# The product with w_in of blocks 1 and 0 by quarters, and the weights' sums made in block 1

## The chip, the core and the metric

The kernel runs on one core of one Trainium2 chip. The metric is device time in microseconds, the median of the runs shown. The engines: PE (TensorE, products; PEld its weight loads), DVE (VectorE), ACT (ScalarE), POOL (GpSimd), SP (SyncE, which issues most DMAs). Each engine takes its instructions in the order of its own queue.

## What is computed

```python
state = gamma * state + k_t v_t          # 4 batches, 8 heads, 768 steps, head size 64
y_t = scale * q_t state
x = y as (3072 tokens, 512)
xn = x / sqrt(mean(x*x) + 1e-6) * rms_g
x = (silu(xn @ w_gate) * (xn @ w_val)) @ w_out        # inner width 1536
h = x @ w_in                                          # 512 -> 1024
e = exp(h - max(h));  sm = e / (sum(e) + 1e-9)
solu = h * sm
ln = (solu - mean(solu)) / sqrt(var(solu) + 1e-6) * g_ln
out = ln @ w_out2                                     # 1024 -> 512
```

All in fp32. On PE a value is split into a high and a low part of type fp32r, and a product takes three matmuls: high by high, high by low, low by high.

## The kernel before

The 3072 tokens go in six blocks of 512. For a block there are these stages. *Attention* (`att_pieces`): per chunk of tokens a group of scores (rq by rk into the PSUM banks SB and YB), masks on DVE (L262, into A), and a group of outputs into the same banks (qd by U, A by rv, then rv by kd for the state); ACT copies the outputs into xT (L317) and squares them (L321). POOL makes qd (L241), kd (L236), the decay of U (L311), the scaling of xT (L322) and zeroes A (L264). *Norm* (`rms_steps`): DVE transposes and sums the squares (L390, L391), PE sums them over partitions (L392), DVE adds the epsilon (L393), POOL takes the root (L394), DVE spreads it (L397), POOL scales xT in four parts (L400), ACT makes the high parts xnh and POOL the low parts xnl (L101). *Values* (`bc_block`): for m from 0 to 11 the products with w_gate (bank GB) and w_val (bank VB), silu on ACT (L819), the multiplication on DVE (L790), a split, and the product with w_out (`cmm`) into the banks X0 to X3, which stand as X_68 to X_71 in the order below.

*Second half.* `de_quarters` (blocks 2 to 5) makes the product with w_in from four quarters of X and of the weights with seven products instead of eight; it needs sums of the weights' quarters: T1 (in two w4 tiles), T2 and T3 (in xnh and xnl, free once the values are done), and T4 (in w2["h"], w2["l"]). `de_block` (blocks 1 and 0) makes it straight, 96 matmuls a block: four groups of 128 tokens, each followed by its softmax. `soft` is the softmax: two maxima on DVE (L989), two exponentials on ACT (L992), on the last group a load of ACT's function table (L995), two multiplications on DVE (L997), and the mean taken off, half on DVE and half on POOL (L1002). `t_tr` transposes the result on PE (L1013), ACT makes the high part (L1016) and DVE the low part (L1017); ACT squares (L1020), and POOL makes the scale of a row with five short instructions (L1024 to L1028), a root among them (L1027). `e_mm` is the product with w_out2, 24 matmuls a group; ACT takes it out with the scale (L1053) and sends it away (L1054).

Block 0's second half runs after block 1's: at the end of block 0's values X goes to DRAM (`x2_store`), and comes back with `x2_load`. So the order is: block 0's values, block 1's values, block 1's second half, block 0's second half, block 2, and so on. Attention and norm of block n+1 are spread over block n's stages: a dictionary `extra` holds functions by (block, slot), `slot(n, s)` runs them, and slots 0 to 34 lie in the values, 35 and more in the second half. For block 2 they lie in the second halves of blocks 1 and 0, from slot 35 on.

The weights' sums: `w2_sums` runs in block 2's values. POOL puts high and low parts together (L601, 128x1024), takes four differences per half (L607), ACT and DVE split them, and SP stores them to `t2scr` in eight stores; `t_load` loads them in each block by quarters.

A scheduler orders the instructions of each engine from the program's order, its own reckoning of time and the marks `issue_after` and `high_priority`.

Of the kernel before, what the change touches and what calls it, by code (L numbers as in the profile page):

```python
# [9 lines left out]
F32 = mybir.dt.float32  # L10
# [13 lines left out]
NK = 4  # L24
# [12 lines left out]
SUMS_AT = [(2, 17), (2, 24)] + [(n, 1 + 6 * i) for n in (3, 4) for i in range(5)]  # L37
W2_SUMS_AT = (2, 9)
FIRST7 = 2
# [3 lines left out]
def retention_moe_kernel(ctx: ExitStack, tc: tile.TileContext, qk0, q2, kt, kv, wpk, w2i, w2o,  # L43
# [550 lines left out]
    def w2_sums(k):  # L594

        W, o = [], []
# [12 lines left out]
        def tied(hi, lo, t):  # L609
            with tc.issue_after(recent["act"].ins), tc.issue_after(recent["dve"].ins):  # L610
                split(hi, lo, t)

        def parts():
            for t in (W[0][:, 0, :], W[1][:, 1, :]):
                o.append(wt("x2", [P, 2, 512], F32R, 4))
                tied(o[-1][:, 0, :], o[-1][:, 1, :], t)

        def parts2():
            tied(w2["h"][:, k, 512:], w2["l"][:, k, 512:], W[1][:, 0, :])
            h, l = (wt("st", [P, 512], F32R, 3) for _ in range(2))  # L620
            tied(h, l, W[0][:, 1, :])
            o.extend((h, l))

        def store():
            for i in range(2):
                nc.sync.dma_start(t2scr[i][:, :, k, :], o[i].bitcast(F32))

        def store2():
            for i in range(2):
                nc.sync.dma_start(t2scr[2][:, i, k, :], o[2 + i].bitcast(F32))  # L630

        def none():
            pass

        return [whole, none, sums, none, parts, parts2, store, store2]
# [172 lines left out]
    def bc_block(n):  # L808
# [28 lines left out]
        if n >= FIRST7:  # L837
            t_load(1, n), t_load(2, n)
# [241 lines left out]
    def t_load(i, n):  # L1080
# [4 lines left out]
        for a in range(2):  # L1085
            nc.sync.dma_start(T1[a].bitcast(F32), t2scr[0][:, a])

    T1 = []

    def de_quarters(n, base):  # L1090

        V, S = nc.vector, nc.scalar

# [6 lines left out]
        for k in range(2):  # L1100
            split(a11[:, 0, k, :], a11[:, 1, k, :], XB[k][:, lo])
            S.copy(s1[:, k, :], XB[k][:, hi])
        for k in range(2):
            V.tensor_tensor(out=s3[:, k, :], in0=XB[k][:, lo], in1=s1[:, k, :], op=ALU.subtract)
        for k in range(2):
            split(xh[:, k, :], xl[:, k, :], XB[2 + k])
# [6 lines left out]
        for k in range(2):  # L1113
            i = V.tensor_tensor(out=s2[:, k, :], in0=XB[2 + k][:, hi], in1=s3[:, k, :], op=ALU.subtract)
# [365 lines left out]
```

## Time and profile before

| | |
|---|---|
| median of 3 runs | 979.44 us (978.98, 979.44, 981.68) |
| profiled execution | 982.31 us |
| its span | 980.4 us, mean granted clock of TensorE 0.991 of full speed |
| DMA over the span | 227.65 MB, mean 232 GB/s |

The profile shows one execution. The span runs from the first to the last instruction. A row of the timeline gives start and duration of an instruction; "x4" joins four in a row, with their time together; what stands in brackets is the idle time of the engine before it, and what ended it. PE's durations overlap, since matmuls are pipelined.

### The profile page before, as it was taken

Reading aid. Unit: us, or ns where it says so; the run is one execution under the profiler, and the core shown is the slowest. Engines: PE = TensorE matmul, PEld = TensorE weight load, DVE = VectorE, ACT = ScalarE, POOL = GpSimd, SP = SyncE. Lnnn points to the kernel's source line nnn. Section 1 sums busy time; section 2 is a strip of 40 time slices with the busy share of each in tenths; the row PEclk is TensorE's granted clock in tenths of the full one; section 3 lists DMA queues with packets and bytes.
Section 4 is the critical chain, followed back from the end, with each engine's and each line's share of the span. In section 5 each row is a group of like instructions: output and inputs, shape, how many; then the busy total and the mean of one; then the engine's idle time right before and its main releaser. Section 6 shows DMA issues by size and latency. Waiting matters only on the chain.

```text
span 980.4 us, 16072 instructions
## 1 busy us (share of the span) xinstructions
PE 966.5 (99%) x5868; PEld 805.4 (82%) x5868; DVE 504.6 (51%) x996; ACT 422.9 (43%) x824; POOL 447.1 (46%) x533
## 2 busy tenths in 40 slices
PE   8899999999999999999999999999999999999998
PEld 7778887888888888888888888888888888899987
DVE  4787785562364653433574233476323456344473
ACT  3766665573335443322455222356312256321354
POOL 6886775572053496443427335528242426300022
PEclk8899999999999999999999999999999999999999
DMA  9699999896612215898833789961698954698501
GB/s 348 225 325 391 347 319 372 324 340 226 200 42 83 70 43 180 279 312 282 294 117 108 278 295 346 300 196 67 205 341 294 322 190 140 230 324 295 193 1 44
DMA packets 94991, 227.65 MB, mean 232 GB/s; under 512 B 10816, under 2 KB 36800, under 8 KB 93888
## 3 DMA queue, kind: packets, MB, share of 16 engines
q1 hardware_dynamic: 86128, 201.44, 60.5%
q10 hardware_dynamic: 8784, 25.17, 6.6%
q8 instruction: 47, 0.77, 0.3%
q14 instruction: 32, 0.26, 0.1%
HBM read 184.63 MB, written 41.94 MB: 231 GB/s over the span
## 4 chain that ended last, share of the span: by engine, by line
PE 90%; POOL 3%; DMA 2%; DVE 2%; ACT 2%; issue 1%; SPq 0%; ACTq 0%; POOLq 0%; DVEq 0%
PE X L771 11%; PE X L773 10%; PE X L772 10%; PE GB L771 7%; PE GB L773 7%; PE GB L772 6%; PE VB L771 6%; PE VB L773 6%; PE VB L772 6%; PE SB L119 3%; PE X L1145 3%; PE GB L1145 2%; PE VB L1145 2%; PE YB L119 2%; PE VB L883 2%; PE YB L883 2%
## 5 line engine op out<-in xcount | busy, mean ns | idle before, releaser
L790 DVE TENSOR_TENSOR f<-VB,f 128x512 f32<-128x512 f32 x60 | 41.4, 690 | 131.4 <-PE VB L773 117.6
L772 PE MATMUL X<-r,wo 128*128 128x512 f32 x260 | 101.7, 391 | 0.0
L773 PE MATMUL X<-r,wo 128*128 128x512 f32 x260 | 101.4, 390 | 0.0
L771 PE MATMUL X<-r,wo 128*128 128x512 f32 x260 | 99.9, 395 | 0.0
L819 ACT ACTIVATE f<-GB 128x512 f32<-128x512 f32 x60 | 35.7, 596 | 144.4 <-PE GB L773 141.4
L100 ACT CAST r<-f 128x512 fp32r<-128x512 f32 x72 | 44.5, 619 | 118.5 <-DVE f L790 100.3
L672 POOL TENSOR_TENSOR st<-st,x 128x512 int32<-128x512 int32 x52 | 70.3, 1356 | 48.7 <-DVE st L671 10.6
L771 PE MATMUL GB<-xnh,w 128*128 128x512 f32 (+1 forms) x220 | 86.6, 394 | 1.5 <-ACT xnh L378 1.0
L771 PE MATMUL VB<-xnh,w 128*128 128x512 f32 (+1 forms) x220 | 86.0, 391 | 0.0
L772 PE MATMUL GB<-xnl,w 128*128 128x512 f32 (+1 forms) x220 | 85.7, 390 | 0.3 <-DVE xnl L101 0.2
L773 PE MATMUL VB<-xnh,w 128*128 128x512 f32 (+1 forms) x220 | 85.6, 389 | 0.0
L772 PE MATMUL VB<-xnl,w 128*128 128x512 f32 (+1 forms) x220 | 85.5, 389 | 0.0
L773 PE MATMUL GB<-xnh,w 128*128 128x512 f32 (+1 forms) x220 | 85.4, 388 | 0.0
L101 DVE TENSOR_TENSOR r<-f,r 128x512 fp32r<-128x512 f32 x72 | 61.7, 858 | 32.6 <-ACT r L100 32.1
L567 POOL TENSOR_TENSOR x<-x 128x512 f32<-128x512 f32 x24 | 31.5, 1319 | 95.6 <-DMA x<-scr 95.3
L101 POOL TENSOR_TENSOR r<-st,r 128x512 fp32r<-128x512 f32 x8 | 10.9, 1360 | 107.1 <-ACT r L100 104.9
L771 PE MATMUL X<-w2oh,r 128*128 128x512 f32 (+1 forms) x144 | 57.2, 397 | 1.1 <-ACT f L1053 0.6
L773 PEld LDWEIGHTS X<-r,wo 128*128 128x128 f32 x260 | 48.8, 188 | 10.2
L771 PEld LDWEIGHTS X<-r,wo 128*128 128x128 f32 x260 | 48.7, 188 | 10.2 <-ACT r L100 0.2
L772 PEld LDWEIGHTS X<-r,wo 128*128 128x128 f32 x260 | 48.8, 188 | 9.9 <-issue 0.2
L773 PE MATMUL X<-w2oh,r 128*128 128x512 f32 (+1 forms) x144 | 55.6, 386 | 0.0
L772 PE MATMUL X<-w2ol,r 128*128 128x512 f32 (+1 forms) x144 | 55.3, 384 | 0.0
(452 smaller groups left out, 2472.7 us busy)
## 6 DMA issues: line engine op xcount, KB each, us to landing
w<-scr SPq DMA_DIRECT2D x96, 512.0 KB, 4.9
wo<-scr SPq DMA_DIRECT2D x59, 512.0 KB, 5.2
x<-in_wpk SPq DMA_DIRECT2D x36, 512.0 KB, 6.2
x<-scr SPq DMA_DIRECT2D x25, 512.0 KB, 6.0
sscr<-x SPq DMA_DIRECT2D x24, 512.0 KB, 7.9
scr<-CV ACTq DMA_DIRECT2D x18, 512.0 KB, 6.2
rv<-in_kv SPq DMA_DIRECT2D x24, 256.0 KB, 4.4
scr<-w ACTq DMA_DIRECT2D x12, 512.0 KB, 4.6
```

What stands on the lines that cost most here:

```text
L100: h = nc.scalar.copy(hi, src)
L101: (lo_eng or nc.vector).tensor_tensor(out=lo, in0=src, in1=hi.bitcast(F32), op=ALU.subtract)
L119: return lambda: nc.tensor.matmul(out, lhsT=lhsT, rhs=rhs, start=start, stop=stop)
L567: nc.gpsimd.tensor_tensor(out=w[:, 0, :], in0=w[:, 0, :], in1=w[:, 1, :], op=ALU.add)
L672: nc.gpsimd.tensor_tensor(out=ti, in0=ti, in1=lo, op=ALU.add)
L771: nc.tensor.matmul(ps, lhsT=lh, rhs=rh, start=start, stop=False)
L772: nc.tensor.matmul(ps, lhsT=lh, rhs=rl, start=False, stop=False)
L773: return nc.tensor.matmul(ps, lhsT=ll, rhs=rh, start=False, stop=stop)
L790: recent["dve"] = nc.vector.tensor_tensor(out=a, in0=GV[1], in1=silu[:, 0, :], op=ALU.mult)
L819: recent["act"] = nc.scalar.activation(s[:, 0, :], GV[0], AF.Silu)
L883: nc.tensor.matmul(ps, lhsT=x, rhs=y[:, k, :], start=start and k + i == 0, stop=k == 1 and i == 2, skip_group_check=True)
L1145: last["mm"] = nc.tensor.matmul(bank, lhsT=x[:, k, ts_], rhs=y[:, k, :], start=start and k + i == 0, stop=k == 1 and i == 2, skip_group_ch ...
```

## The change

`FIRST7` becomes 1, so that blocks 1 and 0 go through `de_quarters` as well; block 0 takes X from DRAM with `x2_back` (two r2 tiles and one x2 tile). `w2_sums` moves to block 1's values, slots 27 to 33; T1 and T4 are split there, T2 and T3 by `w2_rest` into xnh and xnl behind the last product with w_val. They are used from there for blocks 1 and 0 without a load, and `w2_store` stores them once (two stores of 512 KB, two of 1 MB). Block 2's attention pieces are spread over slots 35 to 67 instead of 35 to 56, its norm steps over slots 72 to 77 instead of 57 to 64, and block 2's first weights are loaded at slots 39, 71 and 72. The sums of `SUMS_AT` are four each in blocks 2, 3 and 4.

```diff
--- before.py
+++ after.py
@@ -34,9 +34,9 @@
 CHAIN = 12
 W2_AT = [36 + 2 * j for j in range(16)]
 SEVEN = (5,)
-SUMS_AT = [(2, 17), (2, 24)] + [(n, 1 + 6 * i) for n in (3, 4) for i in range(5)]
-W2_SUMS_AT = (2, 9)
-FIRST7 = 2
+SUMS_AT = [(n, s) for n in (2, 3, 4) for s in ((3, 10, 17, 24) if n == 2 else (1, 8, 15, 22))]
+W2_SUMS_AT = (27, 29)
+FIRST7 = 1
 
 
 @with_exitstack
@@ -593,7 +593,7 @@
 
     def w2_sums(k):
 
-        W, o = [], []
+        W = W2s[k]
 
         def whole():
             for r in (k, k + 2):
@@ -606,33 +606,28 @@
             for out, a, b in ((b11, b12, b11), (b12, b22, b12), (b22, b22, b11), (b21, b21, b22)):
                 nc.gpsimd.tensor_tensor(out=out, in0=a, in1=b, op=ALU.subtract)
 
-        def tied(hi, lo, t):
-            with tc.issue_after(recent["act"].ins), tc.issue_after(recent["dve"].ins):
-                split(hi, lo, t)
-
         def parts():
-            for t in (W[0][:, 0, :], W[1][:, 1, :]):
-                o.append(wt("x2", [P, 2, 512], F32R, 4))
-                tied(o[-1][:, 0, :], o[-1][:, 1, :], t)
-
-        def parts2():
-            tied(w2["h"][:, k, 512:], w2["l"][:, k, 512:], W[1][:, 0, :])
-            h, l = (wt("st", [P, 512], F32R, 3) for _ in range(2))
-            tied(h, l, W[0][:, 1, :])
-            o.extend((h, l))
-
-        def store():
-            for i in range(2):
-                nc.sync.dma_start(t2scr[i][:, :, k, :], o[i].bitcast(F32))
-
-        def store2():
-            for i in range(2):
-                nc.sync.dma_start(t2scr[2][:, i, k, :], o[2 + i].bitcast(F32))
-
-        def none():
-            pass
-
-        return [whole, none, sums, none, parts, parts2, store, store2]
+            w2_tied(w2["h"][:, k, 512:], w2["l"][:, k, 512:], W[1][:, 0, :])
+            w2_tied(T1[0][:, k, :], T1[1][:, k, :], W[0][:, 0, :])
+
+        return [whole, sums, parts]
+
+    W2s = [[], []]
+
+    def w2_tied(hi, lo, t):
+        with tc.issue_after(recent["act"].ins), tc.issue_after(recent["dve"].ins):
+            split(hi, lo, t)
+
+    def w2_rest():
+        for x, w, a in ((xnh, 1, 1), (xnl, 0, 1)):
+            for k in range(2):
+                w2_tied(x[:, k, :], x[:, 2 + k, :], W2s[k][w][:, a, :])
+
+    def w2_store():
+        for a in range(2):
+            nc.sync.dma_start(t2scr[0][:, a], T1[a].bitcast(F32))
+        for i, x in ((1, xnh), (2, xnl)):
+            nc.sync.dma_start(t2scr[i].rearrange("p a k x -> p (a k) x"), x.bitcast(F32))
 
     def load64(key):
         t = wt("x2", [P, 512], I64, 4)
@@ -834,7 +829,9 @@
             else:
                 slot(n, 34)
             w_slot(base + 3 * m + 2)
-        if n >= FIRST7:
+        if n == 1:
+            w2_rest()
+        elif n > 1:
             t_load(1, n), t_load(2, n)
         cmm(n * NM + NM - 1, NM - 1)
 
@@ -1082,14 +1079,22 @@
             nc.sync.dma_start((None, xnh, xnl)[i].bitcast(F32), t2scr[i].rearrange("p a k x -> p (a k) x"))
             return
         T1[:] = [wt("w4", [P, 2, 512], F32R, 4) for _ in range(2)]
-        for a in range(2):
+        for a in range(2 if n > 1 else 0):
             nc.sync.dma_start(T1[a].bitcast(F32), t2scr[0][:, a])
 
     T1 = []
 
+    def x2_back():
+        x23 = wt("x2", [P, 2, 512], F32, 4)
+        X = [wt("r2", [P, 512], F32, 8) for _ in range(2)] + [x23[:, k, :] for k in range(2)]
+        for d in range(NK):
+            nc.sync.dma_start(X[d], x2scr[d])
+        return X
+
     def de_quarters(n, base):
 
         V, S = nc.vector, nc.scalar
+        X = XB if n else x2_back()
 
         def two(t):
             return t.rearrange("p (k i) -> p k i", k=2)
...
         for k in range(2):
-            split(a11[:, 0, k, :], a11[:, 1, k, :], XB[k][:, lo])
-            S.copy(s1[:, k, :], XB[k][:, hi])
+            split(a11[:, 0, k, :], a11[:, 1, k, :], X[k][:, lo])
+            S.copy(s1[:, k, :], X[k][:, hi])
...
@@ -1367,7 +1372,14 @@
             if n == 0:
                 begin, span, r = 0, 30, (31, 32, 33, 33, 33, 33, 34, 34, 35, 35)
             elif n == 1:
-                begin, span, r = 35, 21, (57, 58, 59, 59, 60, 60, 61, 62, 63, 64)
+                begin, span, r = 35, 32, (72, 73, 74, 74, 75, 75, 76, 76, 77, 77)
+                late = [(31, lambda: t_load(0, 1)), (40, w2_store)] \
+                    + [(s, lambda g=2 * NM + i, part=part: w_load(g, part))
+                       for s, i, part in ((39, 0, 0), (39, 0, 1), (71, 1, 0), (72, 1, 1))]
+                for k in range(2):
+                    late += list(zip((W2_SUMS_AT[k], W2_SUMS_AT[k] + 1, W2_SUMS_AT[k] + 4), w2_sums(k)))
+                for s, f in late:
+                    extra.setdefault((1, s), []).append(f)
             else:
                 begin, span, r = 0, 28, (30, 31, 32, 32, 33, 33, 50, 50, 51, 51)
                 extra.setdefault((n, 31), []).append(lambda n=n: t_load(0, n))
@@ -1386,10 +1398,6 @@
                     extra.setdefault((n, s), []).append(f)
             for s, f in zip(r, rms_steps(SB, n + 1)):
                 extra.setdefault((n, s), []).append(f)
-            if n == 2:
-                for k in range(2):
-                    for i, f in enumerate(w2_sums(k)):
-                        extra.setdefault((n, W2_SUMS_AT[k] + i), []).append(f)
             for i, (b, s) in enumerate(SUMS_AT):
                 if b == n:
                     for k, f in enumerate(sums_steps(i // 2, i % 2)):
@@ -1400,12 +1408,9 @@
             x2_store()
             slot(0, 35)
             continue
-        if n >= FIRST7:
-            de_quarters(n, 35)
-            continue
-        de_block(n, XB, 35)
+        de_quarters(n, 35)
         if n == 1:
-            de_block(0, x2_load(), 52)
+            de_quarters(0, 58)
 
 
 # ---- launch: one core; inputs laid out for the chip, tables that depend on shapes alone ----
```

The order of instructions moves with it. First POOL, from the root of block 2's norm (rsum) on. x and f are tiles of block 0's softmax, x_433 and x_434 tiles of the weights' sums, x_464 and x_465 tiles of `sums_steps`. Before:

```order
L394 TENSOR_TENSOR rsum<-rsum,mhalf 128x16
L1025 TENSOR_TENSOR sm_3169<-sm_3169 128x1
L1024 TENSOR_TENSOR sm_3276<-sm_3276 128x1
L1002 TENSOR_SCALAR f_403_3275<-f_403_3275,sm_3276 128x512
L1026 TENSOR_SCALAR sm_3169<-sm_3169 128x1
L400 TENSOR_TENSOR xT<-xT,ssq 128x512 x4
L1027 TENSOR_TENSOR sm_3169<-sm_3169,mhalf 128x1
L264 MEMSET A_3556 64x2x64 x2
L101 TENSOR_TENSOR xnl<-xT,xnh 128x512
L601 TENSOR_TENSOR x_433_3587<-w2ih,w2il 128x1024
L101 TENSOR_TENSOR xnl<-xT,xnh 128x512
```

Now, from the instruction behind the root's followers on:

```order
L999 TENSOR_SCALAR x_423_3316<-x_423_3316,sm_3385 128x512
L1024 TENSOR_TENSOR sm_3333<-sm_3333,mhalf 128x1
L264 MEMSET A_3655 64x2x64 x2
L400 TENSOR_TENSOR xT<-xT,ssq 128x512 x4
L567 TENSOR_TENSOR x_464_3700<-x_464_3700 128x512
L1025 TENSOR_TENSOR sm_3333<-sm_3333 128x1
L567 TENSOR_TENSOR x_465_3702<-x_465_3702 128x512
L1021 TENSOR_TENSOR sm_3413<-sm_3413 128x1
L264 MEMSET A_3850 64x2x64 x2
L1022 TENSOR_TENSOR sm_3385<-sm_3385 128x1
L999 TENSOR_SCALAR f_412_3183<-f_412_3183,sm_3413 128x512
L101 TENSOR_TENSOR xnl<-xT,xnh 128x512
```

Of the weights' sums none stands there now; two instructions of `sums_steps` (L567) and a softmax half (L999, the old L1002) stand between the root and the low parts xnl.

Second PE, at the end of a group of scores (rq by rk) behind the rms sum, in block 0's second half. Before, with the product with w_in (VB) of block 0 behind it:

```order
L119 MATMUL YB<-rq_3026,rk_3027 64x64
L119 MATMUL SB<-rq_3026,rk_3027 64x64
L773 MATMUL VB<-w2ih,x_381_3064 128x512
L771 MATMUL VB<-w2ih,x_382_3069 128x512
L772 MATMUL VB<-w2il,x_382_3069 128x512
L773 MATMUL VB<-w2ih,x_383_3070 128x512
L771 MATMUL VB<-w2ih,x_382_3069 128x512
L772 MATMUL VB<-w2il,x_382_3069 128x512
```

Now:

```order
L119 MATMUL SB<-rq_3107,rk_3108 64x64
L1010 MATMUL X_68<-ident,x_423_3316 128x128 x4
L766 MATMUL X_71<-w2oh,r_443_3484 128x512
L767 MATMUL X_71<-w2ol,r_443_3484 128x512
L1010 MATMUL X_69<-ident,x_423_3316 128x128 x4
L119 MATMUL SB<-A_3655,rv_3109 64x128 x2
L119 MATMUL YB<-A_3649,rv_3109 64x128 x2
L119 MATMUL SB<-A_3655,rv_3109 64x128 x2
L119 MATMUL YB<-A_3649,rv_3109 64x128 x2
L119 MATMUL SB<-rv_3109,kd_3227 64x64 x8
L768 MATMUL X_71<-w2oh,r_444_3485 128x512
```

The group's outputs (A by rv) stand 2 matmuls of 128x512 and two transposed groups behind the scores, where there were 36 matmuls of 128x512 and more. Of the group after it the outputs (qd by U first) follow the scores with no other matmul between, where before at least 12 of 128x512 stood between scores and outputs of any group.

Third ACT, at the table load of block 0's second half. Before:

```order
L1020 ACTIVATE f_403_3275,sm_3276<-f_403_3275 128x1024
L992 ACTIVATE f_410_3370,sm_3372<-VB,sm_3372 128x512
L992 ACTIVATE f_410_3370,sm_3372<-X_68,sm_3372 128x512
L1016 CAST r_415_3399<-X_71 128x512
L995 ACT_TABLE_LOAD
L995 ACTIVATE sm_3372<-sm_3372 128x1
L1053 ACTIVATE f_417_3437<-X_69,sm_3169 128x512
```

Now:

```order
L1051 DMA out<-f_442_3475 128x512
L989 ACTIVATE x_436_3412,sm_3413<-f_412_3183,sm_3413 128x512 x2
L992 ACT_TABLE_LOAD
L992 ACTIVATE sm_3413<-sm_3413 128x1
L1013 CAST r_443_3484<-X_68 128x512
L1013 CAST r_445_3492<-X_69 128x512
L1017 ACTIVATE x_423_3316,sm_3385<-x_423_3316 128x1024
```

The cast of a transposed group (r from X_68) stands behind the table load; before, one of them (r from X_71) stood ahead of it.

## Rows read from the trace of the kernel before

**Rows 1.** share of the span in which each engine is busy, from the page

```profile
PE 966.5 (99%) x5868; PEld 805.4 (82%) x5868; DVE 504.6 (51%) x996; ACT 422.9 (43%) x824; POOL 447.1 (46%) x533
```

**Rows 2.** timeline of TensorE: start, duration, line, operation, tiles (products of block 2)

```profile
470.60 0.39 PE L771 MATMUL GB<-xnh,w 128*128 128x512 f32 x1
...
473.32 0.39 PE L771 MATMUL VB<-xnh,w 128*128 128x512 f32 x1
```

**Rows 3.** GpSimd's groups by shape: line, operation, count | busy us, mean ns | idle before

```profile
L567 POOL TENSOR_TENSOR x<-x 128x512 f32<-128x512 f32 x24 | 31.5, 1319 | 95.6 <-DMA x<-scr 95.3 <-issue 0.2
...
L1002 POOL TENSOR_SCALAR f<-f,sm 128x512 f32<-128x512 f32 x16 | 26.0, 1626 | 0.2 <-DVE sm L1000 0.2
...
L101 POOL TENSOR_TENSOR xnl<-xT,xnh 128x512 fp32r<-128x512 f32 x15 | 20.4, 1377 | 0.3
...
L400 POOL TENSOR_TENSOR xT<-xT,ssq 128x512 f32<-128x512 f32 x16 | 20.2, 1293 | 2.6 <-DVE ssq L397 2.5
...
L394 POOL TENSOR_TENSOR rsum<-rsum,mhalf 128x16 f32<-128x16 f32 x4 | 11.7, 2916 | 16.0 <-DVE rsum L393 16.0
...
L601 POOL TENSOR_TENSOR x<-w2ih,w2il 128x1024 f32<-128x1024 f32 x4 | 10.0, 2496 | 8.8 <-DVE w2il L101 8.1 <-DVE st L101 0.6
...
L575 POOL TENSOR_TENSOR st<-x,x 128x256 f32<-128x256 f32 x12 | 8.9, 738 | 0.0
...
L322 POOL TENSOR_TENSOR xT<-xT,rg_t 128x512 f32<-128x512 f32 x16 | 16.7, 1041 | 5.2 <-ACT xT L317 5.0
...
L1027 POOL TENSOR_TENSOR sm<-sm,mhalf 128x1 f32<-128x1 f32 x24 | 13.9, 580 | 1.3
```

**Rows 4.** timeline of GpSimd around the end of block 1's values

```profile
265.95 0.44 POOL L264 MEMSET A<- 64x128 f32 x2 [36.78 <-PE SB L119]
...
269.19 1.29 POOL L241 TENSOR_TENSOR qd<-rq,qtab_t 128x512 f32<-128x512 f32 x1 [2.80 <-DMA rq<-in_q]
```

**Rows 5.** timeline of TensorE where block 0 ends and block 2 begins

```profile
342.91 0.29 PE L392 MATMUL SB<-rsum,sel_t 128*128 128x16 f32 x2
...
362.78 0.39 PE L771 MATMUL GB<-xnh,w 128*128 128x512 f32 x1
```

**Rows 6.** timeline of VectorE in the same stretch

```profile
343.43 0.17 DVE L393 TENSOR_SCALAR rsum<-SB 128x16 f32<-128x16 f32 x1
...
344.48 0.49 DVE L1002 TENSOR_SCALAR f<-f,sm 128x512 f32<-128x512 f32 x1
...
348.96 0.92 DVE L262 TENSOR_TENSOR A<-YB,mtab_t 128x256 f32<-128x256 f32 x3 [1.63 <-PE SB L119]
...
360.00 2.39 DVE L1002 TENSOR_SCALAR f<-f,sm 128x512 f32<-128x512 f32 x1
```

**Rows 7.** timeline of TensorE: one group of attention products in block 2

```profile
478.85 0.32 PE L119 MATMUL YB<-rq,rk 64*64 64x128 f32 x1
...
479.68 0.50 PE L771 MATMUL X<-r,wo 128*128 128x512 f32 x1
...
483.08 0.32 PE L119 MATMUL SB<-qd,U 64*64 64x128 f32 x1
...
485.17 0.72 PE L1145 MATMUL GB<-w2ih,x 128*128 128x512 f32 x2
```

**Rows 8.** timeline of ScalarE where block 2 ends and block 3 begins

```profile
510.08 0.69 ACT L992 ACTIVATE x<-VB,sm 128x512 f32<-128x512 f32 x1 [0.88 <-DVE sm L990]
...
511.47 0.67 ACT L1053 ACTIVATE f<-GB,sm 128x512 f32<-128x512 f32 x1
...
517.29 0.59 ACT L1016 CAST r<-X 128x512 fp32r<-128x512 f32 x1
...
517.89 1.28 ACT L995 ACT_TABLE_LOAD   x1
```

**Rows 9.** timeline of VectorE in the same stretch

```profile
513.76 1.27 DVE L989 TENSOR_REDUCE sm<-f 128x1 f32<-128x512 f32 x2
```

**Rows 10.** ScalarE's groups by shape

```profile
L317 ACT COPY xT<-YB 64x256 f32<-64x256 f32 x32 | 11.7, 367 | 21.8 <-PE YB L119 21.5
```

More of the change, by code (lines that the diff above doesn't have):

```diff
@@ L1100, in de_quarters @@
         for k in range(2):
-            split(a11[:, 0, k, :], a11[:, 1, k, :], XB[k][:, lo])
-            S.copy(s1[:, k, :], XB[k][:, hi])
+            split(a11[:, 0, k, :], a11[:, 1, k, :], X[k][:, lo])
+            S.copy(s1[:, k, :], X[k][:, hi])
         for k in range(2):
-            V.tensor_tensor(out=s3[:, k, :], in0=XB[k][:, lo], in1=s1[:, k, :], op=ALU.subtract)
+            V.tensor_tensor(out=s3[:, k, :], in0=X[k][:, lo], in1=s1[:, k, :], op=ALU.subtract)
         for k in range(2):
-            split(xh[:, k, :], xl[:, k, :], XB[2 + k])
+            split(xh[:, k, :], xl[:, k, :], X[2 + k])
         def parts(t, eng):
@@ L1113, in de_quarters @@
         for k in range(2):
-            i = V.tensor_tensor(out=s2[:, k, :], in0=XB[2 + k][:, hi], in1=s3[:, k, :], op=ALU.subtract)
+            i = V.tensor_tensor(out=s2[:, k, :], in0=X[2 + k][:, hi], in1=s3[:, k, :], op=ALU.subtract)
         S2 = two(r2()), two(r2())
@@ L1119, in de_quarters @@
             for k in range(2):
-                V.tensor_tensor(out=s1[:, k, :], in0=XB[2 + k][:, hi], in1=s1[:, k, :], op=ALU.add)
+                V.tensor_tensor(out=s1[:, k, :], in0=X[2 + k][:, hi], in1=s1[:, k, :], op=ALU.add)
         S3 = two(r2()), two(r2())
@@ L1128, in de_quarters @@
         for k in range(2):
-            V.tensor_tensor(out=s4[:, k, :], in0=XB[2 + k][:, lo], in1=s2[:, k, :], op=ALU.subtract)
+            V.tensor_tensor(out=s4[:, k, :], in0=X[2 + k][:, lo], in1=s2[:, k, :], op=ALU.subtract)
         S4 = parts(s4, nc.gpsimd)
```

## The prediction, made before the changed kernel was timed

> **What bounds the kernel now.** I read the page first: TensorE is busy 99% of the span, no other engine more than 51% [rows 1]. Busy time of pipelined products overlaps, so I read next, in the timeline, how far apart their starts lie: twelve products of 128x512 go from 470.60 to 473.32, that is 0.2267 us each [rows 2], and the rows of blocks 0 to 2 keep that distance nearly everywhere. So TensorE's queue is the bound in the stages that change. What it loses counts in full, and every wait that it gains counts in full. Then I read the other engines where the change touches them: GpSimd's groups by shape [rows 3], the end of block 1's values [rows 4], the passage from block 0 to block 2 [rows 5, 6], and the passage from block 2 to block 3, which runs by quarters already [rows 7 to 9].
>
> **The change part by part.** (1) *Products removed.* The old product with w_in takes 4 x 24 = 96 products of 128x512 a block, the quarters 14 x 6 = 84. Over two blocks 24 go: 24 x 0.2267 = 5.44 us, all on the bound.
>
> The Trainium skill, "TensorE: Matmul & The Clock Gate", section "Back-to-back issue gap", says that a stream of weight loads and products of 512 columns runs at about 131 ns a product. By that the gain would be an estimated 3.1 us; the trace shows 0.2267 us, and the trace decides.
>
> (2) *Weights' sums on GpSimd in block 1.* Four L601 of 2.5 us and eight of half that size, some 20 us. GpSimd has nothing to do for 36.78 us ahead of 265.95 [rows 4], so I cost it at nothing; if that cover were gone, each microsecond would delay the attention's memsets and masks there. In block 2 the same 20 us leave GpSimd's queue, from under running products: no gain.
>
> (3) *End of block 1's values.* ScalarE gets four more conversions of 0.6 us and VectorE four low parts ahead of the last m's split, and one table load lies between. Bounds 0 and 2.5 us (the four in a row); I take 0.2, since most run while TensorE has the last products with w_val. The 3 MB of stores share SP's queue with the loads of rq and rk; GpSimd waited 2.80 us for rq there before [rows 4]. The fourth quarter's split stands behind that wait on GpSimd, some 15 us ahead of its use, so it costs nothing unless the loads slip by about 3 us more (a rival, below). The first stores have no reader before block 2.
>
> (4) *Block 1's product with w_out.* More attention pieces now fall here. One group has four copies of 0.367 us [rows 10] and two squares of that length on ScalarE, 2.2 us, and they stand ahead of the casts that the last two tokens' groups wait for. In the passage from block 2 to 3 the like cast comes at 517.29 without such copies and no product is late [rows 8]. Bounds 0 and 2.2; I take 1.0. The reload of block 0's X is issued while half of this product still runs, so I cost it at nothing; late, it would hold the first quarter.
>
> (5) *Block 0's product with w_out and the start of block 2.* This is the costly place. Count from the first product of block 0 with w_out. Before, the sum for the rms (L392) ran at 342.91 and block 2's first product with w_gate only at 362.78, 19.9 us later [rows 5]; now the norm of block 2 is asked for with few products left between, and nothing of block 2 can fill in. TensorE's own work up to block 2's second m (120 products, 27.2 us; two groups of scores, 0.83 each; two of outputs, 2.1 and about 1.5 [rows 7]; six groups of transposes, an estimated 0.5 each; the rms sum) is 35.6 us. The waits in it:
>
> a. L392 stands at 9.2 us. VectorE takes 0.52 us to come to L393 [rows 5, 6] and does, behind it, half of a subtraction (0.49) and the last softmax's two reductions, 1.27 [rows 9], to about 11.8. ScalarE: two exponentials, 1.39 from 510.08 to 511.47, the table load 1.28, then the cast of the transposed group, 0.5 to 0.6 [rows 8]: 15.2. TensorE is there at 13.4: about 1.8 us. In block 2 to 3 the cast stands ahead of the table load [rows 8]; here behind it.
>
> b. The second group of scores is followed at once by its outputs. They write the same PSUM banks, so they wait for both masks, 2 x 0.92 us [rows 6]; before, at least 12 products (2.7 us) stood between. About 1.9, and 0.3 for the first group.
>
> So TensorE is late by 4.0 us at least by its neighbours VectorE and ScalarE.
>
> c. GpSimd's queue. The root (L394) starts at 9.95. Behind it, up to the last scale of the outputs (L1025 of the new code, L1028 of the old): two halves of L1002 2 x 1.63, four L400 5.17, two L567 2.64, four low parts 5.51, a qd like L567 1.3, L322 and kd 2.1, four quarter sums L575 2.95, a decay 0.6, three roots L1027 1.74, the first root 2.92 [rows 3]: 28.2, and short ones and memsets of 0.2, some 3. That is 31.2; rows follow each other a little tighter than their durations, so I take 30.6, ending at 40.5. ScalarE then does the last output (0.67 [rows 8]), issues its store and does block 2's first silu, some 0.9 for the two: 42.1. The second m's product with w_gate writes the bank which that silu reads. 42.1 - 35.6 = **6.5 us**, and a. and b. lie inside it.
>
> Bounds: 3.0 (GpSimd in time and the masks partly early) and 9.0. GpSimd's new L567 in this queue need loads issued 2 and 8 us around the count's start; those land in time.
>
> (6) *Later blocks.* Four sums a block in blocks 2 to 4 instead of 2, 5 and 5; eight stores fewer in block 2. All under running products: nothing.
>
> **Sum.** -5.44 + 0.2 + 1.0 + 6.5 = +2.3 us. The profiled execution took 982.31 us (span 980.4), so the like of it would take 984.6. The median of the three runs is 979.44, 2.9 us lower; on it I predict **981.7 us**.
>
> **Rivals.** *R1, the waits do not appear* (the waits of (4) and (5) lie under work that I misjudge). For it: the same tail with quarters runs from block 2 to 3 without a late product [rows 8], and in the old passage TensorE did not wait either [rows 5]. Against it: there the next block's products were ready to fill in. Then -5.44 + 0.4: about 974.4.
>
> *R2, the lock, slower.* In the old passage one L1002 of VectorE took 2.39 us while GpSimd ran an L601, against 0.49 while GpSimd had only the root [rows 6]: 1.9 us. In the new passage VectorE's same operations run under GpSimd's L400, L567 and low parts, ahead of the masks, and GpSimd's queue can be pushed in turn. Every microsecond on that queue is one on TensorE. From 0.64 us of it the loss passes +2.94; with one to two hits the sum is +4.2 to +6.1, 983.6 to 985.5.
>
> The Trainium skill, "SBUF — State Buffer", section "SBUF: two separate sides", says that VectorE and GpSimd share a port pair by an exclusive lock and that the later one blocks fully. The row of 2.39 us agrees with it; whether the passage meets it is what R2 asks.
>
> *R3, slower.* The stores of 3 MB hold rq beyond its 2.80 us [rows 4], and the fourth quarter's low part comes late. From 3 us more on, each costs one: at 5 more, +2 on the sum, 983.7. *That the change does not do what it says* I leave out: the order holds 24 products of this kind fewer.
>
> **How the numbers follow.** Forecast with its own bounds (977.2 up to 983.6, where R2 begins) 0.57; R1 0.14; R2 0.25; R3 0.04. 0.3% is 2.94 us, about what a measurement of this kernel can tell from no change: 976.5 to 982.4. Faster: R1, 0.14. Slower: R2, R3, and the part of the forecast over 982.4, some 0.13: 0.42. Within: 0.44. The range: low from +2.3 with (5) at its lower bound of 3.0 and (4) at nothing, 977.2; high from (5) at 9.0 and (4) at 2.2, 985.4, and R2's end, 985.5. R1 and a little above are left out, under 0.2.
>
> **What would show it.** By quarters, block 1 and 0 each have 12 products fewer; TensorE is without work between block 0's third product with w_out and block 2's second m, first behind the cast after the table load, then behind masks, then behind silu, in all about 6.5 us; GpSimd is without pause there from the root on. A waitless passage would make (5) wrong and R1 right; TensorE late for qd or quarter low parts in block 1 would be R3; a long L999 (the old L1002) on VectorE there R2.

## The result, and the profile after

| kernel | median, us | ratio to the kernel before, with its 95% interval |
|---|---|---|
| before | 979.24 | |
| after | 985.45 (983.37 to 987.71) | 1.0057 (1.0036 to 1.0077) |

The change makes the kernel slower by 0.57%, some 5.6 us. The profiled execution took 984.81 us, with a span of 983.0 us. The span alone misleads by the prologue: up to the first product of block 1's values TensorE took 161.02 us in the trace of before and 158.62 in that of after, and between 157.9 and 162.1 in the others. So I compare one stretch in all traces, from the first product of block 1's values to the first product of block 3: 355.99 us before (161.02 to 517.01), 360.90 after (158.62 to 519.52), **+4.9 us**. Behind it, up to TensorE's last product, all traces agree within 0.6 us. The product with w_out2 is called the product with w_out in the prediction; here it has its own name.

The page's first part, busy time by engine, answers to [rows 1]:

```profile
PE 962.8 (98%) x5844; PEld 800.5 (81%) x5844; DVE 524.2 (53%) x1030; ACT 434.2 (44%) x848; POOL 450.9 (46%) x535
```

TensorE's waits from 180 to 400 us, by what released it (total, count, longest); a wait of TensorE stands nowhere in this stretch of before:

```profile
PE SB L119 <- DVE A L262: 2.0, 1, 2.0
PE X L766 <- ACT r L1013: 1.7, 1, 1.7
PE SB L119 <- POOL A L264: 1.7, 1, 1.7
PE X L1010 <- DVE r L1014: 0.8, 1, 0.8
PE GB L766 <- ACT f L814: 0.4, 1, 0.4
```

Four of the five are attention (masks, A) or the turn from softmax to product (r). In order of time the losses are: 0.8 us at the end of block 1's values, 1.9 at the memset of A in block 1's quarters, 1.5 in block 1's product with w_out2 (the 0.8 at L1014 among it), and 6.4 in the passage, which runs from block 0's first product with w_out2 to the second of the twelve steps m of block 2's values. That is 10.6, less 24 products of 0.2267 us: 5.2 against the 4.9 measured. Of the 6.4, 4.1 are the three waits (1.7, 2.0 and 0.4); most of the rest is work behind the first of them at half clock.

**The passage.** GpSimd's timeline (start, duration, operation, idle time ahead in brackets), from the root of block 2's norm to the last scale of the outputs:

```profile
352.26 3.13 POOL L394 TENSOR_TENSOR rsum<-rsum,mhalf 128x16 f32<-128x16 f32 x1
...
358.34 5.19 POOL L400 TENSOR_TENSOR xT<-xT,ssq 128x512 f32<-128x512 f32 x4
...
372.82 2.54 POOL L101 TENSOR_TENSOR xnl<-xT,xnh 128x512 fp32r<-128x512 f32 x2
...
382.87 0.20 POOL L1025 TENSOR_TENSOR sm<-sm 128x1 f32<-128x1 f32 x1
```

No row between has idle time: 30.8 us without a pause. ScalarE then has the last outputs and block 2's silu (382.32 to 384.27), and TensorE starts the second m at 384.32, 42.2 us from block 0's first product with w_out2.

**End of block 1's values.** VectorE's and GpSimd's rows while the last products with w_val run; TensorE's products behind that low part come 0.3 us late at 221.81 and again at 224.76:

```profile
219.41 2.88 DVE L101 TENSOR_TENSOR r<-f,r 128x512 fp32r<-128x512 f32 x1
```

```profile
219.13 2.60 POOL L601 TENSOR_TENSOR x<-w2ih,w2il 128x1024 f32<-128x1024 f32 x1
```

The same form took 0.69 us on VectorE at 248.74, where GpSimd was idle. The long one ends 0.6 us behind the end of the sum of weights. This is the pattern of [rows 6] (2.39 us beside an L601), in another place than R2 had it.

**Block 1's product with w_out2.** The four copies and two squares of attention stand ahead of ScalarE's cast, as the prediction had it; the cast ends at 309.20. But the transposes at 310.76 wait for VectorE's low part behind it, and between the two VectorE does a sum of attention's squares:

```profile
309.04 1.07 DVE L324 TENSOR_REDUCE ssq<-sq 128x128 f32<-128x512 f32 x1
310.02 1.43 DVE L1014 TENSOR_TENSOR r<-X,r 128x512 fp32r<-128x512 f32 x2
```

**The memset.** DMA queue and GpSimd in block 1's quarters, to hold against [rows 4]:

```profile
260.29 5.96 SPq L219 DMA_DIRECT2D rk<-in_kt  x4
266.29 3.40 SPq L219 DMA_DIRECT2D rq<-in_q  x4
```

```profile
271.49 1.28 POOL L241 TENSOR_TENSOR qd<-rq,qtab_t 128x512 f32<-128x512 f32 x1 [1.95 <-DMA rq<-in_q]
272.73 1.26 POOL L101 TENSOR_TENSOR r<-st,r 128x512 fp32r<-128x512 f32 x1
273.93 0.45 POOL L264 MEMSET A<- 64x128 f32 x2
```

The loads of rk stand behind the stores of the weights' sums; issuing four took 5.96 us (2.49 before), and GpSimd waits for rq ahead of a qd that TensorE needs only for the next chunk. Behind qd and a low part stands the memset of the mask that TensorE needs now.

### The profile page after: what moved, and what is told of

It reads as the page before. It is cut to its first block, busy times and chain, and to the rows that moved or that the text cites. A ratio compares the mean times of both kernels' runs of the same rounds, so it can differ in the third digit from the quotient of the medians.

```text
span 983.0 us, 16074 instructions
## 1 busy us (share of the span) xinstructions
PE 962.8 (98%) x5844; PEld 800.5 (81%) x5844; DVE 524.2 (53%) x1030; ACT 434.2 (44%) x848; POOL 450.9 (46%) x535
## 4 chain that ended last, share of the span: by engine, by line
PE 63%; POOL 5%; DVE 4%; ACT 3%; DMA 1%; issue 1%; ACTq 0%; POOLq 0%
PE X L766 7%; PE X L768 7%; PE X L767 6%; PE GB L766 5%; PE GB L768 4%; PE GB L767 4%; PE X L1150 4%; PE VB L766 4%; PE VB L768 4%; PE VB L767 4%; PE GB L1150 3%; PE VB L1150 3%; PE SB L119 2%; PE VB L880 2%; PE YB L880 2%; PE YB L119 1%
## 5 line engine op out<-in xcount | busy, mean ns | idle before, releaser
L101 DVE TENSOR_TENSOR r<-f,r 128x512 fp32r<-128x512 f32 x72 | 67.8, 943 | 29.8 <-ACT r L100 29.2
L567 POOL TENSOR_TENSOR x<-x 128x512 f32<-128x512 f32 x24 | 30.9, 1289 | 90.7 <-DMA x<-scr 80.0
L101 POOL TENSOR_TENSOR r<-st,r 128x512 fp32r<-128x512 f32 x12 | 16.1, 1340 | 114.3 <-ACT r L100 112.1
```

Source lines behind the costliest of these rows:

```text
L101: (lo_eng or nc.vector).tensor_tensor(out=lo, in0=src, in1=hi.bitcast(F32), op=ALU.subtract)
L567: nc.gpsimd.tensor_tensor(out=w[:, 0, :], in0=w[:, 0, :], in1=w[:, 1, :], op=ALU.add)
```

## Experiments

Stretch is the 355.99 us of before and the 360.90 us of after defined above. It is taken from one execution each, and a fall of TensorE's clock behind a wait can move it by 1.2 to 2.4 us (last section), so smaller differences are read from single waits. Each ratio is to executions of the kernel before taken beside the run, not to 979.24.

| run | median, us | ratio to before (95% interval) | stretch, us |
|---|---|---|---|
| e1_store_later | 986.89 | 1.0061 (1.0041 to 1.0081) | 360.62 |
| e2_no_table_load | 988.70 | 1.0084 (1.0064 to 1.0103) | 363.79 |
| e3_norm_earlier | 979.46 | 0.9997 (0.9983 to 1.0011) | 355.21 |
| e5_three_edits | 981.15 | 1.0006 (0.9993 to 1.0019) | 356.66 |
| e7_no_sums_on_pool | 988.61 | one run | 364.06 |
| e8_longer_norm | 990.72 | one run | 367.09 |
| e9_stores_behind_loads | 984.89 | one run | 361.08 |
| e10_norm_stores_sums | 977.90 | 0.9972 (0.9956 to 0.9988) | 352.70 |
| e11_attention_in_block0 | 983.00 | 1.0027 (1.0009 to 1.0045) | 357.52 |
| e12_spread_wider | 978.98 | 0.9987 (0.9974 to 0.9999) | 354.34 |
| e13_last_chunk_later | 979.09 | 0.9985 (0.9971 to 0.9999) | 354.78 |
| e14_before_late_norm | 984.87 | 1.0041 (1.0026 to 1.0056) | 360.97 |

### Where the norm stands

```diff
-                begin, span, r = 35, 32, (72, 73, 74, 74, 75, 75, 76, 76, 77, 77)
+                begin, span, r = 35, 24, (60, 61, 62, 62, 63, 63, 70, 70, 71, 71)
```

> The changed kernel, with one edit: block 2's attention pieces are spread over slots 35 to 59 instead of 35 to 67, its norm over slots 60 to 63 instead of 72 to 75, and the splits of the normed block over 70 and 71 instead of 76 and 77. So the sum for the rms and the root come at the beginning of block 0's second half, where GpSimd is idle for most of the time. Theory (GpSimd's queue in the passage costs 6.7 us of TensorE): the root (3.1 us), the four scalings (5.2 us) and most of what they push leave the passage, and the passage from block 0's first product with w_out to block 2's second m falls from 42.3 us to 36.5 to 38.5, where at most the wait for the cast behind the table load (1.7 us, with or without a lower clock behind it) is left; total 4 to 6 us lower than the changed kernel, that is between 1.5 us above and 1 us below the kernel before. Rival (the waits are from the cast and the masks, on ScalarE and VectorE, and their order stays): the passage falls by less than 2 us.

The stretch falls by 5.7 us, and the ratio goes from 1.0057 to 0.9997: the theory. The edit also packs the attention pieces closer, since the norm needs their outputs; by itself the run can't part the norm from the attention that leaves the passage with it. The root starts at 324.17 us, beside block 0's product with w_in, where GpSimd of the changed kernel had idle times of 9.36, 6.56 and 5.02 us:

```profile
324.17 2.91 POOL L394 TENSOR_TENSOR rsum<-rsum,mhalf 128x16 f32<-128x16 f32 x1 [0.78 <-DVE rsum L393]
```

The other direction, in the kernel *before*, which has no quarters there:

```diff
-                begin, span, r = 35, 21, (57, 58, 59, 59, 60, 60, 61, 62, 63, 64)
+                begin, span, r = 35, 26, (62, 63, 64, 64, 65, 65, 66, 66, 67, 67)
```

> The kernel before, with no quarters in blocks 1 and 0, and one edit: block 2's attention pieces are spread over slots 35 to 61 and its norm stands at slots 62 to 67 instead of 57 to 64, so that the sum for the rms stands ahead of the last 72 products of block 0 with w_out and w_in or so, about as late as in the changed kernel. Theory (the place of the norm costs, not the quarters): GpSimd's queue from the root on runs for some 28 us with less work of TensorE beside it than that, TensorE waits ahead of block 2's second m, and the stretch from the first product of block 1's values to the first product of block 3 grows from 356.0 us to 359 to 363; ratio 1.003 to 1.007. Rival (the quarters' many small steps on VectorE and ScalarE cost): within 1 us of 356.0, ratio within 0.001 of 1.

The stretch grows by 5.0 us, within the theory. TensorE's waits in that trace (180 to 400 us), one in number, and GpSimd's and ScalarE's rows that lead to it:

```profile
PE GB L771 <- ACT f L819: 3.0, 1, 3.0
```

```profile
352.38 2.93 POOL L394 TENSOR_TENSOR rsum<-rsum,mhalf 128x16 f32<-128x16 f32 x1
...
378.10 0.19 POOL L1028 TENSOR_TENSOR sm<-sm 128x1 f32<-128x1 f32 x1
```

```profile
378.32 0.69 ACT L1053 ACTIVATE f<-X,sm 128x512 f32<-128x512 f32 x1 [2.05 <-POOL sm L1028]
378.91 0.59 ACT L819 ACTIVATE f<-GB 128x512 f32<-128x512 f32 x1
```

So most of the passage's loss needs no quarters at all; a norm in this place makes it in the old code too. Here too the attention pieces move with the norm, but TensorE waits for none of their masks: its one wait is for the end of GpSimd's queue, by way of ScalarE. (There block 2's sums of weights lie in the same queue, four L607 of 1.3 us among them, so the 25.9 us are not made of the same pieces as the 30.8.) The wait is 3.0 us, and the other 2.0 come behind it: twelve products 0.43 us apart instead of 0.2267, at half clock, as the table of stretches shows (stretch, length, TensorE busy and instructions, granted clock, DMA share, GB/s):

```profile
376.00:380.00 4.00, 0.98 (x29) 0.82 0.90 274
380.00:384.00 4.00, 4.00 (x11) 0.50 0.70 243
```

### What sets the end of the passage

```diff
-        if final and n not in (1, NB - 1) and PRE & 1:
+        if final and n not in (0, 1, NB - 1) and PRE & 1:
```

> The changed kernel, with one edit: the last softmax of block 0 doesn't load the function table, so the load (1.28 us) stands directly ahead of block 2's first silu instead of ahead of the cast that TensorE waits for. The order of TensorE, VectorE and GpSimd is unchanged. In the changed kernel TensorE waits 1.74 us for that cast and then runs at a granted clock of 0.61 from 358 to 362, which costs about 1.95 us more. Theory (GpSimd's queue from the root to the last scale of the outputs sets the end of this passage, 30.8 us long whatever TensorE does inside it): the wait for the cast shrinks by about 1.3 us and the clock may stay up, but TensorE then waits the longer for the masks and the scale; and the table load comes on top between the last output and the silu. The passage from block 0's first product with w_out to block 2's second m goes from 42.3 to 43 to 43.6 us; total 0.7 to 1.3 us higher than the changed kernel. Rival (TensorE's waits add up one by one): -1.3 for the cast, -1.95 if the clock stays up, +1.28 at most for the table at the silu: 0 to 2 us lower than the changed kernel, passage 40.3 to 42.3.

Slower by 2.9 us in the stretch; the passage takes 43.7 us instead of 42.2. TensorE waits 1.0 us less for the cast and its clock stays at 1.00 there, yet GpSimd's queue, root to last scale, takes 30.81 us against 30.80 (the run with the stores at slot 51 has 30.82, the one without sums 30.81, the one with the stores moved 30.75). Its rows, and TensorE's wait for silu behind it:

```profile
354.82 3.13 POOL L394 TENSOR_TENSOR rsum<-rsum,mhalf 128x16 f32<-128x16 f32 x1
...
385.44 0.20 POOL L1025 TENSOR_TENSOR sm<-sm 128x1 f32<-128x1 f32 x1
```

```profile
PE GB L766 <- ACT f L814: 1.9, 1, 1.9
```

So the shorter wait for the cast won nothing at the passage's end; the theory holds and its rival falls. The table load on ScalarE then comes in full: from the root to the second m 33.5 us instead of 32.1, and TensorE's first wait for silu is 1.9 instead of 0.4. The rest of the 2.9, about 1.4, is half clock on the products behind that wait (0.59 of full from 388 to 392), which I had not expected. (The 0.56 from 384 to 388 stands behind the masks' wait, ahead of silu.)

> The changed kernel with one size changed: behind two of the four scalings of xT in block 2's norm stands a multiplication by 1.0 on GpSimd (128x512, 1.57 us by the like rows of L999), so 3.1 us more on GpSimd in the passage, and the result is the same. The order of TensorE in the passage is unchanged. Theory (GpSimd's queue sets the end of the passage): from the root's start to the last scale of the outputs 33.9 us instead of 30.8, and the stretch from the first product of block 1's values to the first product of block 3 grows by 3 us, to about 364. Rival (TensorE's single waits on ScalarE and VectorE set it): within 0.7 us of 360.9.

```diff
         nc.gpsimd.tensor_tensor(out=xT[:, k, :], in0=xT[:, k, :], in1=ssq, op=ALU.mult)
+        if longer[0] and k % 2:
+            nc.gpsimd.tensor_scalar(xT[:, k, :], xT[:, k, :], 1.0, None, ALU.mult)
```

The stretch grows by 6.2 us, twice the 3 expected. Some 1.2 of it stand at the very beginning of the stretch, where the edit changes nothing and the clock was at 0.57 from 158 to 162. The added rows took 1.50 us each, but the scheduler put them among the low parts of the normed block, and TensorE now waits for those:

```profile
381.02 0.79 PE L776 MATMUL GB<-xnl,w 128*128 128x512 f32 x1 [4.05 <-POOL xnl L101]
```

The sign and the rival's fall stand; as a measure of a microsecond of GpSimd the run is no good, since the queue's order changed with its length.

### The stores

The first try left the DMA queue as it was: the place in the code went from slot 40 to 51, but the scheduler issued the stores as soon as the sums were there, at the same place.

> The changed kernel, with one edit: the stores of the weights' sums (3 MB) are asked for at slot 51 instead of 40. No engine but the DMA queue has another order. In the changed kernel the loads of rk and rq behind these stores took 5.96 and 3.40 us to issue (2.49 and 2.54 in the kernel before), qd waited for rq, the memset of the mask tile stood behind qd on GpSimd, and the second group of outputs waited 1.68 us for that memset. Theory (the stores delay the loads): the wait of TensorE for the memset in block 1's second half goes, the stretch from the first product of block 1's values to the second m of block 2 falls from 225.7 us to about 223.9, and the time is 1.9 us lower than the changed kernel's, about +3.7 us on the kernel before. Rival (GpSimd is late there through its own work, the low part of a quarter split and qd): wait and stretch stay, within 0.3 us.

```diff
-                late = [(31, lambda: t_load(0, 1)), (40, w2_store)] \
+                late = [(31, lambda: t_load(0, 1)), (51, w2_store)] \
```

So it tells nothing of the stores; that its stretch is 360.62 us against 360.90 shows how well a stretch repeats. The second try ties them behind a load:

```diff
+            with tc.issue_after(recent["rv"].ins):
                 nc.sync.dma_start(t2scr[0][:, a], T1[a].bitcast(F32))
```

> The changed kernel with the stores of the weights' sums (3 MB) placed behind the next two groups of loads of rk, rq and rv in the DMA queue; in the run with slot 51 alone the order of the DMA queue turned out unchanged. TensorE's, VectorE's and ScalarE's orders are unchanged; on GpSimd qd stands four instructions earlier. Theory (the stores delay rq, rq delays qd, qd the memset, the memset TensorE): the loads of rk issue in about 2.5 us instead of 5.96, the wait of TensorE for the memset (1.7 us) in block 1's second half goes, and the stretch from the first product of block 1's values to the first product of block 3 falls from 360.9 to about 359.2 us. Rival (the pieces of attention stand too close together, so that qd is asked for too early whatever the stores do): the wait stays above 1 us.

```profile
259.31 2.50 SPq L219 DMA_DIRECT2D rk<-in_kt  x4
261.85 3.20 SPq L219 DMA_DIRECT2D rq<-in_q  x4
...
280.54 5.50 SPq L219 DMA_DIRECT2D rk<-in_kt  x4
```

```profile
273.81 0.44 PE L119 MATMUL SB<-A,rv 128*64 128x128 f32 x4 [0.89 <-POOL A L264]
```

rk is issued in 2.50 us again, and the four rk behind the stores' new place take 5.50. TensorE's wait falls from 1.68 to 0.89: the stores are about half of it. What makes the other half stays open. In this run qd still waits for rq and stands ahead of the memset, as the rival has it; but with the pieces packed closer still, the wait is 0.6 in the norm's run, where the stores stay, and gone in the run put together below, so closeness alone doesn't make it. Up to block 0's product with w_out2 the trace is 1.0 us ahead of the changed kernel's, but the stretch is the same: the passage takes 1.2 us more. It has the same waits for cast and masks as the changed kernel, but the clock is at 0.63 from 380 to 384 and 0.94 from 384 to 388, where the changed kernel had 1.00 and 1.00.

### The sums on GpSimd

```diff
-                nc.gpsimd.tensor_tensor(out=W[-1].rearrange("p a x -> p (a x)"), in0=w2["h"].bitcast(F32)[:, r, :],
-                                        in1=w2["l"].bitcast(F32)[:, r, :], op=ALU.add)
+                W[-1] = w2["h"].bitcast(F32)[:, r, 0:512].unsqueeze(1).to_broadcast([P, 2, 512])
```

> The changed kernel with one part of the computation left out: GpSimd makes no sums of the weights in block 1's values (four L601 and eight L607, some 20 us of GpSimd); ScalarE and VectorE split a quarter of the weights itself instead, in the same number of instructions, so the output isn't the reference's. In the changed kernel TensorE's products are 0.8 us late in all at 221.81 and 224.76, and VectorE's low part of the activations took 2.88 us at 219.41, against 0.69 for the same form elsewhere, while GpSimd ran an L601 from 219.13 to 221.69. Theory (VectorE is held by GpSimd's sums): the two gaps go, the low part takes 0.7 to 1.0 us, and the stretch from the first product of block 1's values to the first product of block 3 falls from 360.9 us to about 360.0. Rival (the gaps come from the additional conversions and low parts of the split on ScalarE and VectorE): the gaps stay, within 0.2 us.

The two late products are gone, and the low part takes 0.68 us:

```profile
218.93 0.68 DVE L101 TENSOR_TENSOR r<-f,r 128x512 fp32r<-128x512 f32 x1
```

From the first product of block 1's values to the first with w_in it is 104.54 us instead of 105.37: the 0.83 of the theory. The stretch as a whole is 3.2 us *longer*. TensorE came to the memset 0.8 us earlier, the memset did not, and the wait grew from 1.7 to 2.7; behind it the clock fell (the table of stretches), and again behind the passage (0.71 from 384 to 388). A gain in front of a wait that another queue ends is taken back there, here with interest.

```profile
277.00:281.00 4.00, 4.00 (x23) 0.64 0.59 165
```

### Put together

Norm and stores as in the diffs above, and the sums two slots later, where they miss VectorE's low part:

```diff
-W2_SUMS_AT = (27, 29)
+W2_SUMS_AT = (29, 31)
...
-                    late += list(zip((W2_SUMS_AT[k], W2_SUMS_AT[k] + 1, W2_SUMS_AT[k] + 4), w2_sums(k)))
+                    late += list(zip((W2_SUMS_AT[k], W2_SUMS_AT[k] + 1, W2_SUMS_AT[k] + 3), w2_sums(k)))
```

> The changed kernel with block 2's norm at the beginning of block 0's second half, the stores of the weights' sums behind the next two groups of loads, and the weights' sums two slots later (29 and 31). Theory (each place costs by itself, so what is left of the norm's run falls further): the run with the norm alone had 355.2 us from the first product of block 1's values to the first product of block 3, with late products of 0.8 us at the end of block 1's values, 0.8 at the memset, 1.7 at the transposes of block 1's last softmax, 0.5 and 0.6 in the passage. The first two go: 353.6 us, 2.4 us less than the kernel before (356.0), ratio about 0.9975. Rival (the waits move to the next late one): 355 us, ratio 0.999.

977.90 us, ratio 0.9972: this beats both kernels, by a little more than the theory said (353.6 us in the stretch), with 3.3 us less in the stretch than before, 8.2 less than the change as it was. The end of block 1's values (104.52 us) and the memset lose nothing any more; what is left of TensorE's waits from 180 to 400:

```profile
PE X L1012 <- DVE x L1001: 1.1, 1, 1.1
PE GB L768 <- ACT f L816: 0.5, 1, 0.5
```

An earlier run put together the norm's edit, the stores' slot (which moves nothing) and the table load's edit:

> The changed kernel with the three edits together: stores of the weights' sums at slot 51, norm of block 2 at the beginning of block 0's second half, no load of the function table in block 0's last softmax. Theory (each of the three places costs by itself): -1.9 for the stores, -4 to -6 for the norm, and with GpSimd's queue gone the table load costs nothing at the first silu, since a whole product with w_val of 2.7 us lies between, so another 1.3 to 1.7 us off: 7 to 9.5 us lower than the changed kernel, 2 to 4 us lower than the kernel before (24 products of 0.2267 us are 5.44 us, less what block 1 keeps losing). Rival (the waits only move): no more off than the norm alone, about the time of the kernel before.

That run shows the table load from the other side: with GpSimd's queue gone from the passage, it makes TensorE wait 1.9 us for block 2's first silu, 1.5 us in the stretch compared with the norm's run. I had it as a gain. It belongs where the changed kernel has it.

Three more tries moved the attention's chunks to save the 1.1 us, and each lost in the stretch (4.8, 1.6 and 2.1 us); for the last two the intervals of the ratios overlap with that of the run they start from. Their places of the eight pieces and of the ten steps of the norm, one after the other:

```diff
+                places = (35, 38, 42, 46, 58, 60, 63, 65); r = (66, 67, 68, 68, 69, 69, 72, 72, 73, 73)
+                places = (35, 38, 41, 45, 49, 54, 59, 62); r = (64, 65, 66, 66, 67, 67, 68, 68, 69, 69)
+                places = (35, 38, 41, 45, 48, 51, 58, 61); r = (62, 63, 64, 64, 65, 65, 68, 68, 69, 69)
```

> The run with norm, stores and sums moved (352.7 us in the stretch from the first product of block 1's values to the first product of block 3), with one more edit: the last two chunks of block 2's attention stand at slots 58 to 65, in block 0's products with w_in, where GpSimd and VectorE have idle time, instead of 48 to 59, the norm at 66 to 69, the splits of the normed block at 72 and 73. Theory (attention beside a product with w_out delays the softmax: 1.1 us at the transposes of block 1's last softmax): that wait goes, 351.5 us, unless the later norm brings GpSimd's queue back into the passage. Rival (GpSimd's queue in the passage decides; the norm is later by 6 slots): the wait ahead of block 2's second m grows by more than the 1.1 us won, 353 to 356 us.

> The run with norm, stores and sums moved (352.7 us in the stretch), with the attention pieces at 35, 38, 41, 45, 49, 54, 59 and 62 (the third and fourth chunk a little later), the norm at 64 to 67, and the splits of the normed block at 68 and 69 instead of 70 and 71. Theory (the third chunk's outputs and the fourth chunk's masks stand between the steps of block 1's last softmax): the 1.1 us at its transposes goes, and the wait ahead of block 2's second m (0.5) shrinks: 351.2 us. Rival: the wait moves to another softmax, 352.7 us within 0.5.

> The run with norm, stores and sums moved (352.7 us in the stretch), with only the fourth chunk of block 2's attention later (58 and 61 instead of 55 and 59), the third chunk's outputs a slot earlier (51), the norm at 62 to 65 and the splits of the normed block at 68 and 69 instead of 70 and 71. TensorE's order changes little. Theory (the earlier splits of the normed block shorten GpSimd's queue in the passage): the wait ahead of block 2's second m (0.5) goes, the 1.1 us at block 1's last softmax stays: 352.2 us. Rival (that wait comes from ScalarE's last output and silu alone): 352.7 us.

The first has the root at 337.27 us instead of 321.03, and GpSimd's queue is back in the passage: the rival, and more than it said (+4.8). The second and third lie outside both of their expectations. The second lost its 1.1 us at block 1's last softmax but waits 1.0 for a cast in block 0 instead, with shorter ones beside it; the third keeps the 1.1 and has the same 1.0 in block 0. In both the splits of the normed block stand two slots earlier, in front of block 0's product with w_out2, and I did not separate which of the moves makes that wait.

## Why the prediction was right, and where it was not

The measured 985.45 us lies in the range, at its very end (985.5). Its sum had the right sign and its largest term held, but the size did not: +2.3 us was forecast, about 5 came, so that it is slower by more than 0.3% and not within it, the likelier of the two by a little (0.44 against 0.42). That the range holds it is in part luck: its upper end came from a passage of 9.0 us, which did not appear (6.4). What filled the gap were terms (2), (3) and (4), 3.0 us too low together, and the range was not built from the first two.

- *Term 1, products*: right. 24 fewer, at 0.2267 us.
- *Term 5, the passage*: right, in size and in mechanism. GpSimd's queue was forecast at 30.6 us and took 30.8, the passage at 42.1 and took 42.2. It was right that the waits for cast (1.7 forecast as 1.8) and masks (2.0, 1.9) lie inside it: removing 1.0 of the first left the queue at 30.81. And moving the norm, with the attention ahead of it, gave 5.7 us back.
- *Term 3, the end of block 1's values and the loads of rk and rq behind it*: mis-sized, 0.2 against the memset's 1.9. The step that failed is "The fourth quarter's split stands behind that wait on GpSimd, some 15 us ahead of its use". That split was in time; I named one instruction behind the wait for rq, and the memset of A stood behind it as well, with no slack. I had R3's mechanism with a chance of 0.04 and the wrong victim. And the stores explain only about half; the cause of the rest stays open.
- *Term 2, the sums on GpSimd at nothing*: failed, 0 against the 0.8 at the end of block 1's values. The cover was read as GpSimd's idle time (36.78 us); what costs is not GpSimd's queue but VectorE held by it, the mechanism that R2 placed in the passage only. There it may show too: an L999 of VectorE took 1.33 us at 361.04, beside GpSimd's L400, where the like row of before took 0.49 [rows 6]. GpSimd's queue runs on without a pause, so the passage's end doesn't show it.
- *Term 4*: 1.0 forecast, 1.5 measured, within its bounds. The copies and squares ahead of the cast were forecast; the sum of the squares on VectorE (1.07 us, L324) ahead of the low part was left out.
- *R1* is out: the waits appeared. *R2* gives the right number, 983.6 to 985.5, for a wrong place.
- *Term 6, later blocks at nothing*: right within what the traces resolve; from the end of the stretch to TensorE's last product 459.8 us before, 460.1 after.

The Trainium skill, "TensorE: Matmul & The Clock Gate", section "Back-to-back issue gap", with its 131 ns a product, put the removed products at an estimated 3.1 us; by that the sum would have come to an estimated 4.6, nearer to the measured 5 by accident. The trace does not agree: the products stand 0.2267 us apart as before.

## What to carry to other kernels

A step that is moved later takes its whole tail with it: count, on the engine that runs it, all that is queued from its first instruction to the last one that the bottleneck needs, and compare that with the bottleneck's own work left; here 30.8 us, and 1.3 of ScalarE behind it, against some 26 (the prediction's 35.6 less the 10 ahead of the root). Behind an added wait look at every instruction in that queue, with the slack of each, not only at the one that seems next. And an engine's idle time is not a free place for work if its neighbour, held while it works, stands ahead of the bottleneck.

## What was not expected of the hardware

TensorE's granted clock fell to its half level (1.2 instead of 2.4 GHz) behind some waits of 1.7 to 3.0 us, and not behind others of the same length. In the changed kernel it fell behind the cast's wait of 1.74 us and not behind the masks' 2.0:

```profile
358.00:362.00 4.00, 4.00 (x39) 0.61 0.38 102
...
380.00:384.00 4.00, 2.16 (x48) 1.00 0.86 307
384.00:388.00 4.00, 3.68 (x16) 1.00 0.83 272
```

(A figure between half and full is a window in which the clock changed; the products at half clock lie 0.43 us apart.) With the stores moved, and the order of TensorE unchanged, it fell behind both:

```profile
380.00:384.00 4.00, 2.97 (x36) 0.63 0.89 313
```

With the edit that moved nothing (the stores' slot alone) it fell only behind the second, to 0.57 from 384 to 388. So equal orders of work get different clocks, and a passage with waits varies by it: free where another engine sets the passage's end (the changed kernel and the run without the table load have the same queue on GpSimd, with and without the fall behind the cast), 1.2 to 2.4 us where TensorE's products follow. Why one wait and not the other I did not find out.
